# Attention and a gated convolution on one core: the convolution's wrapped columns, and a new order for every instruction

## The chip, the core and the metric

The kernel runs on one core of a Trainium2 chip. The core has five engines that run side by side, each with its own instruction queue that it works off strictly in order: TensorE (PE in the profile; PEld are its weight loads), VectorE (DVE), ScalarE (ACT), GpSimd (POOL) and SyncE (SP). SP issues transfers and does no arithmetic; POOL and ACT issue some as well. An instruction waits on semaphores for what other engines or transfers have to finish first. The metric is the time of one execution on the device, in microseconds (us); lower is better.

## The reference

Two layers follow each other. The first is attention with pooled keys and values, the second a feed-forward block whose hidden values are gated by a convolution along the sequence.

```python
# q, k, v: batch 8, heads 8, sequence 576, head size 64
k_p = k.reshape(B, H, 72, 8, D).mean(axis=3)          # 72 pooled keys per head
v_p = v.reshape(B, H, 72, 8, D).mean(axis=3)
scores = matmul(q, k_p.T) / sqrt(D)
scores -= max(scores, axis=-1)
attn = exp(scores); attn /= sum(attn) + 1e-9
x = matmul(attn, v_p)                                  # heads side by side: 8 x 576 x 512
h = maximum(x @ w_in, 0)                               # 512 -> 1024
conv_out[s] = w[0] * h[s-1] + w[1] * h[s] + w[2] * h[s+1]   # per feature, zeros beyond the ends
out = (h * sigmoid(conv_out)) @ w_out                  # 1024 -> 512
```

Inputs and output are float32; the kernel computes in bf16 with float32 sums.

## The kernel before

Batches are taken in pairs, called groups: g0 holds batches 0 and 1, g3 batches 6 and 7. A group has nine tiles of 128 rows (t0 to t8; t4 is shared by both batches; g0 has a tenth).

*Attention* (`add_att`), per tile: scores on PE (L607 by quarters of the array, L620 with the whole array), maximum on DVE (L633), the maximum taken off on DVE (L645; for g0 on PE, L653), exponential on ACT (L682), a turn of the result (g0 and g1: PE at L692 and a copy at L706; g2 and g3: a transposing transfer from SP), the product with the values on PE (L717), a reciprocal (L730) and the division, on DVE at L745 or as eight narrow ACT instructions at L738. The result is turned again into `xT` (PE and a copy at L762 and L770, or a transfer). Ahead of that, keys are pooled and turned (L431 in halves, L441 in quarters of the array, copies at L456, L483, L504), queries turned (L541, L545, copy at L559), and values folded by DVE in three additions (L511) and spread by a mask (L515).

*Feed-forward* (`add_ffn`), per batch: the first matrix product on PE (L775), a ReLU on ACT into `hT` (L784), and then for each quarter of the work, which is four of the eight blocks of 128 features (`f4`), the convolution in one of two ways.

- On DVE, for the seven quarters in `TAPS` (batches 4 to 6 whole and the first half of batch 7): two instructions per block (L911) add the neighbours, an ACT instruction (L921) squashes.
- On PE, for the other nine quarters (`ffn_conv`, L939): diagonal 64 by 64 matrices times shifted columns of `hT`, in four quarters of the array at once; ACT squashes (L964).

Then DVE multiplies gate and hidden values (L989), and PE makes the output tiles with the second matrix (`add_out`, L997), which ACT or DVE copies out (L1008) for a store.

*Wrapped columns.* The sequence is stored in nine runs of 64 columns, so that the neighbour of the last column of one kind lies at the far end of the tile. `hT` has spare columns on both sides. For batches 4 to 7 (`WRAP`) POOL copies 63 columns to each side (`ffn_wrap`, L859 and L860), two blocks at a time, so that a shifted read is one piece. Where there is no wrap, `conv_todo(False)` cuts the shifted reads into pieces instead. Before, batch 7's second quarter, the last that PE convolves, reads wrapped columns: 24 matmuls per pair of blocks, after POOL's copies.

*The order.* Nothing is scheduled while the kernel is built: `ORDER` lists every operation by its number with the engine it goes to, `FORMS` tells which shape PE uses where there is a choice, and `PLACES` which buffer an operation gets. Numbers of -1 are filler matmuls (L424), of which 40 are used. `Graph.order` reads these lists; since every engine works in order, they set what waits behind what.

*Loads.* POOL issues the loads of queries (L284), keys (L284, L291), values (L317, L320) and weights (L327, L335) in list order, so a load that waits for its buffer holds back those behind it.

```python
        for n in self.ORDER:
            o = spares.pop(0) if n < 0 else self.ops[n // 2]
            o.engine = list(o.engines)[0 if n < 0 else n % 2]
```

Of the kernel before, what the change touches and what calls it, by code (L numbers as in the profile page):

```python
# [12 lines left out]
ACT = mybir.ActivationFunctionType  # L13
# [20 lines left out]
class Graph:  # L34
# [148 lines left out]
def kernel(  # L183
# [1125 lines left out]
    def add_ffn(b, w):  # L1309
# [28 lines left out]
        for f4 in range(n_fb // 4 if b in Graph.WRAP else 0):  # L1338
            n = Graph.WRAPS
            for lo in range(4 * f4, 4 * f4 + 4, n):  # L1340
                o = add({"POOL": (0.6, 1.0, 0, 1.5)[n - 1]}, w, lambda lo=lo, n=n: ffn_wrap(b, lo, lo + n), uses=[htok[b]],
                        after=[o for fb in range(lo, lo + n) for o in relu[fb]] + [ends])
                for fb in range(lo, lo + n):
                    wraps[fb] = o
# [151 lines left out]
```

## Time and profile before

| what | us |
|---|---|
| median of 3 runs | 217.48 (216.86 to 217.99) |
| the profiled execution, whole | 217.29 |
| its span, first to last instruction | 215.4 |
| PE busy | 202.8 |
| DVE busy | 190.8 |
| ACT busy | 164.8 |
| POOL busy | 45.7 |

The span is what the engines' rows cover; the profiled execution's own time is 1.89 us longer. A row of a group names the source line, the engine, the operation, what it writes and reads, the shape and how often; then the busy time in us and the mean length of one in ns, and then idle time just before it with what ended that. A busy PE is not a PE at its peak, since matmuls overlap. A row of the timeline gives start, length and, in brackets, idle time before it.

### The profile page before, as it was taken

What the parts mean: (1) busy time and instruction counts of PE and PEld (TensorE: products, weight loads), DVE (VectorE), ACT (ScalarE), POOL (GpSimd) and SP (SyncE); (2) the same over time, 40 slices, a digit from 0 to 9 for tenths busy, and PEclk for the clock granted to TensorE, in tenths of its full rate; (3) what the DMA queues carried; (4) which work ended last, traced back from release to release, by engine and by line L of the source; (5) the groups of instructions that cost most, each with busy time, mean ns of one, the idle gap of its engine ahead of it and who ended that gap; (6) DMA issues with size and microseconds to landing.
All of it is one profiled execution on the core that took longest, in us unless ns stands there. A gap on an engine that the chain in (4) does not pass through costs nothing.

```text
span 215.4 us, 6639 instructions
## 1 busy us (share of the span) xinstructions
PE 202.8 (94%) x2728; PEld 136.1 (63%) x2728; DVE 190.8 (89%) x338; ACT 164.8 (77%) x331; POOL 45.7 (21%) x78
## 2 busy tenths in 40 slices
PE   4979999999999999989999999999999999989992
PEld 1546778775688877756867775566466556735451
DVE  7779989999999989979999999999999999998521
ACT  2527767998898878977996996999989988968220
POOL 8824130443102012000000142040210411281000
PEclk9999999999999999999999999999999999999999
DMA  6999999999999998965788686565567553320985
GB/s 209 215 205 207 208 205 208 208 207 206 207 248 208 205 141 127 174 150 61 141 116 121 138 115 132 74 139 116 103 134 170 125 109 79 73 46 3 241 257 185
DMA packets 48833, 33.46 MB, mean 155 GB/s; under 512 B 28300, under 2 KB 43812, under 8 KB 48804
## 3 DMA queue, kind: packets, MB, share of 16 engines
q0 software_dynamic: 15216, 15.40, 43.8%
q1 hardware_dynamic: 32592, 16.20, 36.9%
q10 hardware_dynamic: 996, 1.45, 2.4%
q8 instruction: 21, 0.34, 0.6%
q14 instruction: 8, 0.07, 0.1%
HBM read 32.52 MB, written 9.44 MB: 195 GB/s over the span
## 4 chain that ended last, share of the span: by engine, by line
PE 58%; DVE 17%; ACT 9%; issue 3%; POOLq 1%; DMA 1%; POOL 1%; DVEq 0%; ACTq 0%
PE psum L997 23%; PE psum L775 18%; PE psum L717 4%; PE psum L939 4%; DVE negm L633 4%; DVE sd L645 3%; DVE x L745 3%; DVE gT L989 2%; ACT hT L784 2%; PE psum L762 2%; DVE gT L981 2%; ACT gT L964 2%; PE psum L607 2%; PE psum L692 2%; ACT tg L964 1%
## 5 line engine op out<-in xcount | busy, mean ns | idle before, releaser
L775 PE MATMUL psum<-xT,w_in_sb 128*128 128x288 bf16 x512 | 71.6, 286 | 0.5 <-ACT tg L964 0.3
L997 PE MATMUL psum<-w_out_sb,gT 128*128 128x512 bf16 (+1 forms) x296 | 68.0, 374 | 1.3 <-DVE sd L645 1.1
L775 PEld LDWEIGHTS <-w_in_sb 128*128 128x128 bf16 x512 | 48.3, 98 | 16.7 <-issue 1.2
L784 ACT ACTIVATE hT<-psum 128x576 bf16<-128x576 f32 x64 | 41.2, 664 | 8.3 <-PE psum L775 7.8
L997 PEld LDWEIGHTS <-gT 128*128 128x128 bf16 x296 | 27.4, 98 | 28.2 <-DVE sd L645 1.3
L633 DVE TENSOR_REDUCE negm<-psum 128x8 f32<-128x576 f32 (+2 forms) x37 | 27.4, 749 | 3.0 <-PE psum L607 1.6
L859 POOL COPY hT<-hT 128x126 bf16<-128x126 bf16 x16 | 10.6, 661 | 90.0 <-ACT hT L784 73.0
L911 DVE SCALAR_TENSOR_TENSOR tg<-hT,ratio 128x576 f32<-128x576 bf16 x28 | 22.5, 814 | 1.2 <-ACT gT L921 0.5
L911 DVE SCALAR_TENSOR_TENSOR tg<-hT,ratio,tg 128x576 f32<-128x576 bf16 x28 | 22.7, 821 | 0.8
L921 ACT ACTIVATE gT<-tg,ratio 128x576 bf16<-128x576 f32 x28 | 21.4, 790 | 0.5 <-DVE tg L911 0.2
L989 DVE TENSOR_TENSOR gT<-gT,hT 128x2304 bf16<-128x2304 bf16 x16 | 21.3, 1345 | 0.2
L645 DVE TENSOR_TENSOR sd<-psum,negm 128x576 f32<-128x576 f32 x27 | 20.1, 754 | 0.9
L682 ACT ACTIVATE e<-sd 128x576 bf16<-128x576 f32 x27 | 18.8, 701 | 1.8 <-DVE sd L645 1.7
L738 ACT ACTIVATE x<-psum,r 128x64 bf16<-128x64 f32 x80 | 17.6, 341 | 1.7 <-DVE r L730 1.7
L745 DVE TENSOR_TENSOR x<-psum,r 128x512 bf16<-128x512 f32 (+1 forms) x27 | 18.4, 686 | 0.6
L717 PE MATMUL psum<-vm,eT 128*128 128x65 bf16 (+5 forms) x240 | 18.5, 222 | 0.3 <-DMA eT<-e 0.3
L939 PE MATMUL psum<-hT,dw 64*64 64x288 bf16 (+2 forms) x560 | 17.5, 258 | 1.1 <-POOL hT L859 0.7
L717 PEld LDWEIGHTS <-eT 128*128 128x128 bf16 (+1 forms) x240 | 14.8, 100 | 4.0 <-DMA eT<-e 0.6
L939 PEld LDWEIGHTS <-dw 64*64 64x64 bf16 x560 | 13.8, 107 | 5.0 <-issue 4.3
L1008 ACT COPY osb<-psum 128x512 f32<-128x512 f32 x26 | 15.4, 601 | 0.9 <-PE psum L997 0.9
L964 ACT ACTIVATE gT<-psum 128x576 bf16<-128x576 f32 x18 | 11.6, 656 | 5.4 <-PE psum L939 5.4
L424 PE MATMUL psum<-gT 128*128 128x448 bf16 x40 | 12.6, 415 | 2.9 <-DVE gT L1106 2.8
(96 smaller groups left out, 243.1 us busy)
## 6 DMA issues: line engine op xcount, KB each, us to landing
out_dram<-osb SPq DMA_DIRECT2D x54, 128.0 KB, 2.5
v<-in_v_dram POOLq DMA_DIRECT2D x8, 512.0 KB, 14.8
qp<-in_q_dram POOLq DMA_DIRECT2D x7, 576.0 KB, 18.7
kk<-in_k_dram POOLq DMA_DIRECT2D x3, 1152.0 KB, 16.5
out_dram<-qp ACTq DMA_DIRECT2D x10, 128.0 KB, 2.9
hT<-in_k_dram SPq DMA_DIRECT2D x2, 576.0 KB, 5.1
w_in_sb<-in_moe_w_in_dram POOLq DMA_DIRECT2D x2, 512.0 KB, 15.8
w_out_sb<-in_moe_w_out_dram POOLq DMA_DIRECT2D x1, 1024.0 KB, 18.9
```

Of the source, the lines that this page charges most:

```text
L633: nc.vector.tensor_reduce(out=a["m"][0:rows], in_=a["s"][0:rows, :, 0:2 * KW].rearrange("p a (h s) -> p a h s", s=Sp), axis=AX.X, op=OP.ma ...
L645: nc.vector.tensor_tensor(out=a["d"][0:rows], in0=a["s"][0:rows, :, 0:2 * KW].rearrange("p a (h s) -> p a h s", s=Sp), in1=a["m"][0:rows]. ...
L682: nc.scalar.activation(out=dst, in_=src, func=ACT.Exp,)
L717: nc.tensor.matmul(out=a["o"][lo:hi, h // 4, (h % 4) * (D + 1):(h % 4 + x1 - x0) * (D + 1)], lhsT=a["eT"][:, j, lo:hi], rhs=buf("vm", b)[: ...
L745: nc.vector.tensor_tensor(out=a["x"][0:rows].rearrange("p (a h d) -> p a h d", a=2, d=D), in0=ov[:, :, :, 0:D], in1=r[0:rows].unsqueeze(3) ...
L775: nc.tensor.matmul(out=banks(ps)[:, j, 0:SC], lhsT=w_in_block(dc, fb), rhs=buf("xT", g)[:, dc, i * S + j * SC:i * S + (j + 1) * SC], start ...
L784: nc.scalar.activation(out=h_of(b)[:, fb].rearrange("p (a s) -> p a s", a=2), in_=banks(ps)[:, :, 0:SC], func=ACT.Relu, scale=1.0 if (b, f ...
L911: nc.vector.scalar_tensor_tensor(out=acc, in0=h, scalar=w, in1=acc if tap else mid, op0=OP.mult, op1=OP.add)
L921: nc.scalar.activation(out=gate, in_=acc_of(b, fb, ps), func=squash(b, fb), scale=ratio[:, 1, fb:fb + 1])
L939: nc.tensor.matmul(out=banks(pss[r ^ c])[c * D:(c + 1) * D, j, lo:hi], lhsT=dw[r * D:(r + 1) * D, tap * n_fb + fb, :], rhs=hT[r * D:(r + 1 ...
L989: nc.vector.tensor_tensor(out=gate, in0=gate, in1=h_of(b)[:, four], op=OP.mult)
L997: nc.tensor.matmul(out=bank(ps)[0:rows, columns], lhsT=buf("gT", g)[:, fb, t * P:t * P + rows], rhs=w_out_sb[:, fb, columns], start=(fb == 0),
```

## The change

Four edits go together.

1. PE's convolution always uses the cut pieces: batch 7's second quarter goes from 24 to 32 matmuls per pair of blocks and depends on the ReLUs alone.
2. Wraps are made only where DVE convolves, fourteen instead of sixteen.
3. A wrap can be put on ACT; the new order puts three of the fourteen there (batch 4 blocks 6 and 7, batch 6 blocks 6 and 7, batch 7 blocks 2 and 3).
4. `ORDER`, `FORMS` and `PLACES` are new throughout. Beside the sequence of everything, this changes which engine some operations run on, and on POOL's queue the sequence of the loads.

```diff
     ORDER = (
-        0, 12, 10, 24, 16, 4, 44, 28, 8, 36, 14, 32, 46, 40, 64, 38, -1, -1, 21, 3,
...
+        0, 10, 24, 16, 4, 44, 28, 8, 36, 12, 14, 32, 46, -1, -1, -1, -1, -1, -1, 42,
...
-    def ffn_wrap(b, lo, hi):
+    def ffn_wrap(b, lo, hi, copy):
         t = buf("hT", b)[:, lo:hi]
-        nc.gpsimd.tensor_copy(out=t[:, :, 1:TB], in_=t[:, :, S:S + TB - 1])
-        nc.gpsimd.tensor_copy(out=t[:, :, TB + S:TB + S + TB - 1], in_=t[:, :, TB + 1:2 * TB])
+        copy(out=t[:, :, 1:TB], in_=t[:, :, S:S + TB - 1])
+        copy(out=t[:, :, TB + S:TB + S + TB - 1], in_=t[:, :, TB + 1:2 * TB])
...
-        hT, todo = buf("hT", b), conv_todo(b in Graph.WRAP)
+        hT, todo = buf("hT", b), conv_todo(False)
...
         for f4 in range(n_fb // 4 if b in Graph.WRAP else 0):
+            if (b, f4) not in Graph.TAPS and b not in Graph.SIXTEEN:
+                continue
             n = Graph.WRAPS
             for lo in range(4 * f4, 4 * f4 + 4, n):
-                o = add({"POOL": (0.6, 1.0, 0, 1.5)[n - 1]}, w, lambda lo=lo, n=n: ffn_wrap(b, lo, lo + n), uses=[htok[b]],
+                o = add({"POOL": (0.6, 1.0, 0, 1.5)[n - 1], "ACT": 0.43}, w, None, uses=[htok[b]],
                         after=[o for fb in range(lo, lo + n) for o in relu[fb]] + [ends])
+                o.emit = lambda lo=lo, n=n, o=o: ffn_wrap(b, lo, lo + n, nc.gpsimd.tensor_copy if o.engine == "POOL" else nc.scalar.copy)
...
-            conv = add({"PE": 0.64 if b in Graph.WRAP else 0.66}, w + 6 * f2 + Graph.QCONV + nudge("c", 4 * b + f2), lambda f2=f2, cbs=cbs: ffn_conv(b, f2, cbs),
-                       after=([wraps[fbs[0]]] if fbs[0] in wraps else relu[fbs[0]] + relu[fbs[1]]) + dwo, uses=cbs + tg + [htok[b], gtok[g]],
-                       mode=QUARTER, count=48 if b in Graph.WRAP else 64)
+            conv = add({"PE": 0.66}, w + 6 * f2 + Graph.QCONV + nudge("c", 4 * b + f2), lambda f2=f2, cbs=cbs: ffn_conv(b, f2, cbs),
+                       after=relu[fbs[0]] + relu[fbs[1]] + dwo, uses=cbs + tg + [htok[b], gtok[g]],
+                       mode=QUARTER, count=64)
```

What the new order moves, counted in the instructions of both kernels (before, after):

| operation | DVE | ACT |
|---|---|---|
| division of a tile (L745; eight narrow ones at L738) | 25, 23 | 10, 12 tiles |
| turn copy 128x640 (L706) | 7, 3 | 10, 14 |
| turn copy 128x320 (L706) | 0, 1 | 2, 1 |
| key copy 64x288 (L456) | 0, 2 | 2, 0 |
| key copy 128x576 (L504) | 1, 0 | 1, 2 |
| query copy 128x1152 (L559) | 2, 4 | 8, 6 |
| query copy 128x512 (L559) | 1, 0 | 1, 2 |
| output copy 128x512 (L1008, last group) | 3, 4 | 5, 4 |
| wrap copies (L859, L860; before all on POOL, 32, after 22) | - | 0, 6 |

On PE: L431 36 to 54, L441 72 to 36, L541 108 to 126, L545 216 to 180, L607 320 to 352, L620 64 to 56, L939 560 to 576 matmuls. POOL's loads before: values 0, rest of queries 0, keys 1, queries 1, input weights, queries 2, values 1, values 2, keys 2 and 3, queries 3, queries 4, output weights, values 3, values 4, and on. After: rest of queries 0, values 0, keys 1, queries 1, queries 2, input weights, values 1, keys 2 and 3, queries 3, queries 4, output weights, values 2, values 3, keys 4 and 5, and on. At the end of DVE's queue the products of batch 6 (L989) are now followed by six of batch 7's convolution steps (L911) instead of five.

More of the change, by code (lines that the diff above doesn't have):

```diff
@@ L72 @@
     ORDER = (
[54 rows of a table removed]
[54 rows of a table added]
     )
     FORMS = (
-        0, 0, 0, 0, 1, 1, 1, 0, 0, 0, 1, 1, 1, 0, 1, 0, 1, 0, 0, 0, 0, 1, 1, 1, 1, 0, 0, 1, 0, 0, 0, 1, 1, 1, 1, 1, 1, 1, 0, 0,
+        1, 1, 0, 0, 1, 0, 1, 0, 0, 1, 0, 0, 1, 1, 0, 0, 1, 0, 0, 0, 0, 1, 1, 1, 0, 0, 0, 1, 1, 0, 0, 1, 1, 1, 0, 1, 1, 1, 0, 1,
     )
     PLACES = (
[18 rows of a table removed]
[18 rows of a table added]
     )
```

142 rows, old and new, of tables (ORDER, PLACES) are left out of this document.

## The prediction

> **What bounds the kernel now.** I read the page's first part, then busy time by stretch, then the timeline around the last wait, then the groups by shape.
>
> ```profile
> span 215.4 us, 6639 instructions
> PE 202.8 (94%) x2728; PEld 136.1 (63%) x2728; DVE 190.8 (89%) x338; ACT 164.8 (77%) x331; POOL 45.7 (21%) x78
> ```
>
> TensorE (PE) and VectorE (DVE) are both nearly full over the span, so neither share alone names the bound. The next rows give stretches: start and end, then busy time of PE, its weight loads, DVE, ScalarE (ACT) and GpSimd (POOL).
>
> ```profile
> 0.00:27.00 27.00, 22.53 (x335) 14.31 (x335) 22.28 (x62) 13.78 (x24) 13.87 (x29) 1.00 1.08 209
> 27.00:125.00 98.00, 95.72 (x1712) 71.37 (x1709) 91.89 (x167) 82.31 (x154) 13.29 (x19) 1.00 1.04 169
> 125.00:190.00 65.00, 64.47 (x550) 40.37 (x549) 63.22 (x94) 59.55 (x140) 14.54 (x26) 1.00 0.56 116
> 190.00:195.00 5.00, 3.96 (x54) 2.12 (x56) 4.58 (x5) 2.51 (x5) 3.98 (x4) 1.00 0.00 0
> 195.00:201.40 6.40, 6.40 (x42) 2.93 (x31) 6.08 (x9) 4.93 (x9) 0.00 (x0) 1.00 0.31 72
> 201.40:215.40 14.00, 9.73 (x53) 5.00 (x51) 2.76 (x5) 1.76 (x3) 0.00 (x0) 1.00 0.78 230
> ```
>
> From 27 to 190 us PE idles 2.28 + 0.53 = 2.8 us and DVE 6.1 + 1.8 = 7.9 us; ACT has 15.7 us free until 125 and 5.5 us from there to 190. The granted clock is 1.00 in every stretch, so it plays no part. The next rows are the timeline at the end (start, length, what; in brackets the idle time before it and who ended it).
>
> ```profile
> 190.41 2.62 DVE L989 TENSOR_TENSOR gT<-gT,hT 128x2304 bf16<-128x2304 bf16 x2
> 190.44 2.74 POOL L859 COPY hT<-hT 128x126 bf16<-128x126 bf16 x1 [0.88 <-ACT hT L784]
> 193.13 0.81 POOL L860 COPY hT<-hT 128x126 bf16<-128x126 bf16 x1
> 193.23 0.43 PE L939 MATMUL psum<-hT,dw 64*64 64x288 bf16 x6 [0.71 <-POOL hT L859]
> 193.99 1.41 PE L939 MATMUL psum<-hT,dw 64*64 64x288 bf16 x38 [0.33 <-POOL hT L860]
> 194.12 0.29 POOL L860 COPY hT<-hT 128x126 bf16<-128x126 bf16 x1
> 194.21 0.82 DVE L911 SCALAR_TENSOR_TENSOR tg<-hT,ratio 128x576 f32<-128x576 bf16 x1 [0.42 <-POOL hT L859]
> 195.41 15.72 PE L997 MATMUL psum<-w_out_sb,gT 128*128 128x512 bf16 x80
> 198.72 2.63 DVE L989 TENSOR_TENSOR gT<-gT,hT 128x2304 bf16<-128x2304 bf16 x2
> ```
>
> Two paths reach the end together. PE runs its last 80 output matmuls without a break until 195.41 + 15.72 = 211.13; a copy and a store fill the remaining 4.27 us. The last five tiles are 40 of 72 full matmuls' worth (16 of the 80 are half wide), 8.73 us, so PE reaches them at 202.40. They need DVE's last gate products, which end at 198.72 + 2.63 = 201.35. DVE is thus only 1.05 us ahead of PE: a gain must be made on both.
>
> **The change, part by part.** The sum is against this execution: 215.4 + 1.89 around the span = 217.29 us, 0.19 below the median of 217.48.
>
> *The convolution.* Only the last quarter (batch 7, features 512 to 1023) still used wrapped columns on PE. Its two convolutions go from 24 to 32 matmuls each, with the same columns of result. The wrapped ones took 1.41 us for 38, 37 ns each, so 24 take 0.89; the unwrapped ones follow:
>
> ```profile
> 42.50 0.92 PE L939 MATMUL psum<-hT,dw 64*64 64x288 bf16 x32
> ```
>
> So 0.92 against 0.89, +0.06 for two; I take 0.1, with ends 0 and 0.5 (a further eight at 29 ns each, twice). [...]
>
> *Its wrap copies go.* The convolution waits for ACT's activations alone. The two PE waits above, 0.71 + 0.33 = 1.04 us, and DVE's 0.42 us go. Late next is the last activation on ACT, behind one wrap, two squashings and a copy; PE has half an output tile and a convolution (1.7 us) to cover them.
>
> *The other wraps.* Fourteen remain, eleven on POOL and three on ACT. A POOL copy takes 0.29 us alone and 2.74 beside DVE's products. [...] Five fewer pairs on POOL free nothing on DVE that these rows show; I take 0. Those on ACT follow ACT's own ReLUs and wait for no other engine; behind each stand squashings and ReLUs, whose delay is in rival A.
>
> *Work moved from DVE to ACT* (counts from the two engine orders, lengths from these groups, mean ns after the comma):
>
> ```profile
> L745 DVE TENSOR_TENSOR x<-psum,r 128x512 bf16<-128x512 f32 x25 | 17.0, 686 | 0.5
> L706 DVE COPY eT<-psum 128x640 bf16<-128x640 bf16 x7 | 3.4, 482 | 0.2 <-PE psum L692 0.2
> L1008 DVE COPY qp<-psum 128x512 f32<-128x512 f32 x3 | 2.0, 689 | 5.1 <-DMA out_dram<-qp 5.1
> L559 DVE COPY qT<-psum 128x1152 bf16<-128x1152 bf16 x2 | 1.5, 748 | 0.0
> L504 DVE CAST kT<-psum 128x576 bf16<-128x576 f32 x1 | 0.8, 751 | 0.0
> L559 DVE COPY qT<-psum 128x512 bf16<-128x512 bf16 x1 | 0.4, 418 | 0.0
> L738 ACT ACTIVATE x<-psum,r 128x64 bf16<-128x64 f32 x80 | 17.6, 341 | 1.7 <-DVE r L730 1.7
> L706 ACT COPY eT<-psum 128x640 bf16<-128x640 bf16 x10 | 6.7, 696 | 2.2 <-PE psum L692 2.0
> L559 ACT COPY qT<-psum 128x1152 bf16<-128x1152 bf16 x8 | 9.0, 1128 | 0.1
> L483 ACT CAST kT<-psum 64x288 bf16<-64x288 f32 x8 | 3.0, 391 | 0.1
> L921 ACT ACTIVATE gT<-tg,ratio 128x576 bf16<-128x576 f32 x28 | 21.4, 790 | 0.5 <-DVE tg L911 0.2
> ```
>
> DVE before its last product: two divisions less (-1.37), four turn copies less (-1.93), one short one more (+0.30, by half the width of 482 plus a little), one key copy less (-0.75), two 64x288 key copies more (+0.90; this shape is not on DVE before, ends 0.39 and 0.75 each, I take 0.45 as the nearest row is ACT's same shape), two query copies more and one short one less (+1.50 - 0.42). Sum -1.77, with ends -1.9 and -1.2. The extra output copy (0.69) lies after the last product.
> ACT: sixteen narrow divisions more (17.6/80 = 0.22 each, +3.5), four turn copies (+2.8), six wrap copies (between 0.22 and 0.39 each, 0.3, +1.8), two query copies less (-2.3), smaller ones -0.6: +5.2 us. The cover is the 21 us that ACT has free from 27 to 190; without it each of these microseconds would be paid.
>
> *PE's choice of shapes* (keys and queries turned in halves or quarters, scores by rows):
>
> ```profile
> L431 PE MATMUL psum<-gT,kk 128*64 128x144 bf16 x36 | 1.5, 229 | 0.0
> L441 PE MATMUL psum<-gT,kk 64*64 64x72 bf16 x72 | 0.9, 198 | 0.0
> L541 PE MATMUL psum<-ident,qp 128*64 128x128 bf16 x108 | 4.3, 227 | 1.5 <-DMA qp<-in_q_dram 1.3
> L545 PE MATMUL psum<-ident,qp 64*64 64x64 bf16 x216 | 2.9, 195 | 0.1
> L607 PE MATMUL psum<-kT,qT 64*64 64x72 bf16 x320 | 6.0, 199 | 0.0
> L620 PE MATMUL psum<-kT,qT 128*128 128x144 bf16 x64 | 6.5, 226 | 0.2 <-ACT gT L964 0.2
> ```
>
> Busy time over count gives the price: +18 of L431 (0.75), -36 of L441 (-0.45), +18 of L541 (0.72), -36 of L545 (-0.48), +32 of L607 (0.60), -8 of L620 (-0.81): +0.33 us. The 40 filler matmuls stay. In the tail two stores move from ACT's queue to SP's; the last tile keeps one store on each queue per half, so I leave the 4.27 us as they are.
>
> *The start.* On POOL's queue the rest of batch 0's queries now goes ahead of its values, and DVE's first three score maxima ahead of the first fold of the values.
>
> ```profile
> 11.94 1.35 DVE L511 TENSOR_TENSOR v<-v 128x1280 bf16<-128x1280 bf16 x2 [1.74 <-DMA v<-in_v_dram]
> 15.35 1.42 DVE L633 TENSOR_REDUCE negm<-psum 128x8 bf16<-128x576 f32 x2 [0.35 <-PE psum L620]
> ```
>
> DVE's wait of 1.74 us for the values goes; late next are the scores of the first tile, which waited behind it for about as long. Between 0 and 1.74 + 0.35 = 2.1, I take 0.6, nearer the low end since PE and ACT must first make those scores.
>
> *The loads.* Batch 2's values are issued after the output weights instead of before batch 3's queries; batch 2's queries ahead of the input weights.
>
> ```profile
> 50.32 0.74 POOL L284 DMA_DIRECT2D qp<-in_q_dram  x1 [1.46 <-DMA w_out_sb<-in_moe_w_out_dram]
> 53.25 0.74 POOL L317 DMA_DIRECT2D v<-in_v_dram  x1 [2.19 <-DMA v<-in_v_dram]
> 55.01 0.69 DVE L745 TENSOR_TENSOR x<-psum,r 128x512 bf16<-128x512 f32 x1
> ```
>
> Up to batch 3's values both orders have loaded the same bytes: output weights are down by 50.3 us and those values by 53.2. Batch 2's now take the place between, so they land at about 50.3. DVE folds them where the division at 55.01 stood, about 2.2 us earlier by then (a lighter queue and the start), 52.8. The margin is 2.5 us, so I take 0; it costs what goes beyond.
>
> *The sum.* DVE's last product: 201.35 - 1.77 - 0.6 - 0.42 + 0.35 (it now waits for two squashings of 0.79 that end late) = 198.9. PE's arrival at the last five tiles: 202.40 - 1.04 - 0.6 + 0.1 + 0.33 = 201.2, and less again by what it idled on a late DVE from 27 to 190: between 0 and 2.8, half, 1.4, giving 199.8. PE is the later. 199.8 + 8.73 + 4.27 + 1.89 = **214.7 us**. If PE wins back none of its idle time, 216.1; if all of it, DVE decides: 198.9 + 0.1 + 8.73 + 4.27 + 1.89 = 213.9. With the start at its best on both, 212.4. A change of 0.5%, 1.1 us, is about what the three runs (216.86 to 217.99) can tell from none.
>
> **The rivals.**
> *A, ACT becomes the late engine (slower).* Its extra 5.2 us stand in the same queue as the ReLUs that PE and DVE wait for, and from 125 to 190 it is 92% busy already. For it: 59.55 of 65 us. Against: most of the extra work lies before 125 us, where 15.7 us are free. It decides where more than half of the 5.2 us, the 2.6 us that the sum gains, comes on the path: all of it gives 214.7 + 5.2 = 219.9, three quarters 218.6. Chance 0.24.
> *B, batch 2's values come late (slower).* The queue waits, ahead of them, for query buffers that PE must empty. If that issue slips, DVE stands still in order, and everything behind it. It decides from a landing at 52.8 + 2.6 = 55.4; at 58 us the time is 219.9. The rows have the landing 5 us before that. Chance 0.08.
> *C, what the waits gave up is idle elsewhere (no change).* All orders are new, and DVE's 7.9 us and PE's 2.8 us of idle time from 27 to 190 are in many short waits, none of which carries over. With 2.5 us more of them on the path, 217.2. Chance 0.15.
>
> **How the numbers follow.** The forecast, 212.4 to 216.1, has 0.53; A 0.24, B 0.08, C 0.15. C is within 0.5%, A and B are slower. The likeliest case gives the time. For eight in ten the range leaves out a tenth at each end: low 212.5, high 220.0, where A and B in full end.
>
> **What would show it.** Right: no POOL wait before the last convolution, 64 matmuls there in under 2 us; DVE busy about 1.1 us less in all and its first 1.74 us wait gone; ACT busy near 170; the last 40 output matmuls starting near 199.8. Wrong: a DVE wait of over 2 us on values or scores between 40 and 80 us (B); DVE or PE rows idle on ACT's ReLUs for over 3 us in all (A); a stop of over 1 us ahead of the last five tiles would say that DVE, not PE, sets the end.

## The result, and the profile after

The changed kernel takes 218.93 us (median of 12 runs; 218.64, and 217.94 to 219.99, without the first) against 217.57 us for the kernel before beside it: a ratio of 1.0066, 95% interval 1.0037 to 1.0096. It is slower, and the whole interval lies above 1; 214.7 us was forecast. On a second chip the unchanged file gave 219.18 us and 1.0109 (1.0066 to 1.0151). The first of the twelve, which was the profiled one, took 336.67 us at a mean granted clock of 0.56 and is left out of the ratio, so the trace read here is that of another execution of the same kernel, 218.56 us.

Lines of its page: span, busy times, and the shares of the chain that ended last.

```profile
span 216.6 us, 6657 instructions
PE 203.6 (94%) x2732; PEld 136.8 (63%) x2732; DVE 189.6 (88%) x336; ACT 168.5 (78%) x353; POOL 38.9 (18%) x68
PE 58%; ACT 12%; DVE 12%; DMA 10%; issue 3%; POOL 1%; SPq 0%; DVEq 0%; ACTq 0%
```

Transfers make 10% of the chain, before 1%: 4% are transfers of turned exponentials, 4% loads of values, 2% transfers of the turned output `xT`. Busy time by stretch, columns as before:

```profile
0.00:27.00 27.00, 24.29 (x373) 15.19 (x374) 22.03 (x61) 15.11 (x25) 11.20 (x22) 1.00 1.08 204
27.00:125.00 98.00, 93.52 (x1647) 69.85 (x1646) 88.81 (x161) 82.87 (x167) 15.08 (x24) 1.00 1.04 172
125.00:190.00 65.00, 64.91 (x558) 41.10 (x557) 63.67 (x96) 60.59 (x147) 12.63 (x22) 1.00 0.59 114
190.00:195.00 5.00, 5.00 (x82) 2.98 (x81) 5.00 (x6) 4.92 (x10) 0.00 (x0) 1.00 0.23 52
195.00:201.40 6.40, 6.40 (x31) 2.92 (x30) 5.98 (x9) 3.24 (x6) 0.00 (x0) 1.00 0.19 44
```

From 190 us on PE's rows are full and no wait for POOL is left, as forecast. The loss is in the second row: PE idles 98.00 - 93.52 = 4.48 us there, before 2.28, and DVE 9.19, before 6.11. The chain shows where (start, length, what):

```profile
93.99 4.38 DMA eT<-e
98.37 0.05 issue
98.42 1.28 PE psum L717 x18
...
103.18 3.57 DMA eT<-e
106.75 0.05 issue
106.80 0.53 PE psum L717 x6
...
200.73 1.37 DVE gT L989
202.10 0.05 issue
202.15 8.84 PE psum L997 x48
```

The products with the values wait for turned exponentials. PE's timeline has the same two stops (idle time before in brackets):

```profile
98.42 1.28 PE L717 MATMUL psum<-vm,eT 128*128 128x130 bf16 x18 [2.19 <-DMA eT<-e]
106.80 0.53 PE L717 MATMUL psum<-vm,eT 128*128 128x130 bf16 x6 [1.23 <-DMA eT<-e]
```

SP issues these transfers; its own timeline, first of the changed kernel, then of the one before (L553 sends a batch's queries, L701 an exponential tile, L1020 stores):

```profile
85.00 1.12 SPq L1020 DMA_DIRECT2D out_dram<-osb  x2
86.31 7.58 SPq L553 DMA_TRANSPOSE qT<-qp  x1
93.99 3.49 SPq L701 DMA_TRANSPOSE eT<-e  x2
97.54 1.22 SPq L1020 DMA_DIRECT2D out_dram<-osb  x2
98.87 2.80 SPq L553 DMA_TRANSPOSE qT<-qp  x1
```

```profile
86.27 1.11 SPq L1020 DMA_DIRECT2D out_dram<-osb  x2
87.49 2.72 SPq L701 DMA_TRANSPOSE eT<-e  x2
90.31 4.08 SPq L553 DMA_TRANSPOSE qT<-qp  x1
98.27 3.27 SPq L701 DMA_TRANSPOSE eT<-e  x2
```

Before, two exponential tiles went out first, at 87.49, and the queries behind them. After, the queries of batch 6 stand first, and to issue their transfer holds SP for 7.58 us; the same instruction needs 2.80 us at 98.87. What ran at that time is on POOL's queue:

```profile
65.96 0.79 POOL L284 DMA_DIRECT2D qp<-in_q_dram  x1
74.06 1.01 POOL L291 DMA_DIRECT2D kk<-in_k_dram  x1 [7.31 <-PE psum L470]
82.53 0.77 POOL L317 DMA_DIRECT2D v<-in_v_dram  x1 [7.46 <-DVE vm L515]
83.29 0.56 POOL L320 DMA_DIRECT2D v<-in_v_dram  x1
83.85 0.76 POOL L284 DMA_DIRECT2D qp<-in_q_dram  x1
```

The row at 83.85, now the last load of all, is the one of batch 7's queries. Before, it went out at 50.32. Now it stands behind the values of batch 7 (82.53), which wait 7.46 us for their buffer. The list of transfers gives it 10.1 us to land (KB, then us), so until 93.95, just as SP comes free:

```profile
qp<-in_q_dram POOLq DMA_DIRECT2D x1, 576.0 KB, 10.1
```

The end lost time too. SP's timeline there, after and before (`qp` holds the last group's output tiles):

```profile
192.34 3.92 SPq L1020 DMA_DIRECT2D out_dram<-osb  x4
201.68 1.11 SPq L1020 DMA_DIRECT2D out_dram<-qp  x2
202.83 4.75 SPq L1020 DMA_DIRECT2D out_dram<-osb  x6
207.80 6.10 SPq L1020 DMA_DIRECT2D out_dram<-qp  x8
```

```profile
198.15 1.11 SPq L1020 DMA_DIRECT2D out_dram<-qp  x2
199.30 6.99 SPq L1020 DMA_DIRECT2D out_dram<-osb  x10
206.39 5.86 SPq L1020 DMA_DIRECT2D out_dram<-qp  x6
```

After, SP issues nothing from 196.26 to 201.68: it waits for a tile's copy, and finished tiles of group 2 stand behind. From 201.6 us on, 26 transfers are left to issue on SP and ACT, before 22. PE's last matmul ends at 210.97 (before 211.13), the span 5.63 us later, before 4.22.

The sum of the traced execution beside the forecast: PE reaches the last five tiles at 202.15 instead of 199.8 (+2.35), they take 8.82 instead of 8.73, the end behind them 5.63 instead of 4.27 (+1.36), and 1.96 lies around the span instead of 1.89: 218.56 against 214.7.

### The profile page after: what moved, and what is told of

Same layout as the page of the kernel before. It is cut to its first block, busy times and chain, and to the rows that moved or that the text cites. A ratio compares the mean times of both kernels' runs of the same rounds, so it can differ in the third digit from the quotient of the medians.

```text
span 334.7 us, 6637 instructions
## 1 busy us (share of the span) xinstructions
PE 324.9 (97%) x2712; PEld 183.6 (55%) x2732; DVE 193.5 (58%) x336; ACT 175.3 (52%) x353; POOL 34.1 (10%) x68
## 4 chain that ended last, share of the span: by engine, by line
PE 97%; issue 1%; ACT 0%; DVE 0%; DVEq 0%
PE psum L775 33%; PE psum L997 32%; PE psum L939 7%; PE psum L717 7%; PE psum L424 4%; PE psum L692 3%; PE psum L762 2%; PE psum L541 2%; PE psum L620 2%; PE psum L607 2%; PE psum L653 1%; PE psum L431 1%; PE psum L545 1%; PE psum L493 0%; PE psum L470 0%
## 5 line engine op out<-in xcount | busy, mean ns | idle before, releaser
L775 PE MATMUL psum<-xT,w_in_sb 128*128 128x288 bf16 x512 | 118.9, 415 | 0.0
L997 PE MATMUL psum<-w_out_sb,gT 128*128 128x512 bf16 (+1 forms) x276 | 111.6, 569 | 4.0 <-issue 2.9
L775 PEld LDWEIGHTS <-w_in_sb 128*128 128x128 bf16 x512 | 66.2, 134 | 40.0 <-issue 7.1
L997 PEld LDWEIGHTS <-gT 128*128 128x128 bf16 x296 | 37.1, 129 | 59.6 <-issue 55.7
L730 DVE RECIPROCAL r<-psum 128x8 f32<-128x8 f32 (+1 forms) x37 | 7.6, 206 | 52.2 <-PE psum L717 32.0
L911 DVE SCALAR_TENSOR_TENSOR tg<-hT,ratio 128x576 f32<-128x576 bf16 x28 | 22.2, 816 | 15.0 <-ACT gT L921 12.8
L1008 ACT COPY osb<-psum 128x512 f32<-128x512 f32 x26 | 15.2, 589 | 27.3 <-PE psum L997 21.5
L717 PE MATMUL psum<-vm,eT 128*128 128x65 bf16 (+5 forms) x240 | 27.8, 284 | 0.0
L717 PEld LDWEIGHTS <-eT 128*128 128x128 bf16 (+1 forms) x240 | 21.4, 126 | 7.3 <-issue 3.6
L939 PE MATMUL psum<-hT,dw 64*64 64x288 bf16 (+2 forms) x576 | 25.3, 343 | 0.0
L738 ACT ACTIVATE x<-psum,r 128x64 bf16<-128x64 f32 x96 | 20.9, 334 | 5.3 <-DVE r L730 3.7
L911 DVE SCALAR_TENSOR_TENSOR tg<-hT,ratio,tg 128x576 f32<-128x576 bf16 x28 | 22.3, 812 | 0.6
L989 DVE TENSOR_TENSOR gT<-gT,hT 128x2304 bf16<-128x2304 bf16 x16 | 21.4, 1346 | 0.5 <-ACT gT L921 0.3
L939 PEld LDWEIGHTS <-dw 64*64 64x64 bf16 x576 | 16.9, 130 | 8.1 <-issue 3.4
L859 POOL COPY hT<-hT 128x126 bf16<-128x126 bf16 x11 | 3.9, 353 | 160.4 <-ACT hT L784 127.4
L745 DVE TENSOR_TENSOR x<-psum,r 128x512 bf16<-128x512 f32 (+1 forms) x25 | 16.9, 684 | 0.5
```

The costliest lines, as they stand in the source:

```text
L717: nc.tensor.matmul(out=a["o"][lo:hi, h // 4, (h % 4) * (D + 1):(h % 4 + x1 - x0) * (D + 1)], lhsT=a["eT"][:, j, lo:hi], rhs=buf("vm", b)[: ...
L738: nc.scalar.activation(out=a["x"][0:rows, n * D:(n + 1) * D], in_=ov[:, n // 4, n % 4, 0:D], func=ACT.Identity, scale=r[0:rows, n // 4, n ...
L775: nc.tensor.matmul(out=banks(ps)[:, j, 0:SC], lhsT=w_in_block(dc, fb), rhs=buf("xT", g)[:, dc, i * S + j * SC:i * S + (j + 1) * SC], start ...
L911: nc.vector.scalar_tensor_tensor(out=acc, in0=h, scalar=w, in1=acc if tap else mid, op0=OP.mult, op1=OP.add)
L939: nc.tensor.matmul(out=banks(pss[r ^ c])[c * D:(c + 1) * D, j, lo:hi], lhsT=dw[r * D:(r + 1) * D, tap * n_fb + fb, :], rhs=hT[r * D:(r + 1 ...
L989: nc.vector.tensor_tensor(out=gate, in0=gate, in1=h_of(b)[:, four], op=OP.mult)
```

## The experiments

Every kernel was timed beside the kernel before. The order is edited where `Graph.order` returns it: `done` is the list of operations in the sequence of `ORDER`, with shapes and buffers already given, so to move an entry changes its place on its own engine's queue and nothing else. The added lines shift line numbers by one to four (L701 becomes L702 to L705).

**The changed kernel once more, the convolution alone, the wraps back on POOL.**

```diff
-        hT, todo = buf("hT", b), conv_todo(b in Graph.WRAP)
+        hT, todo = buf("hT", b), conv_todo(False)
...
-                       after=([wraps[fbs[0]]] if fbs[0] in wraps else relu[fbs[0]] + relu[fbs[1]]) + dwo, uses=cbs + tg + [htok[b], gtok[g]],
+                       after=relu[fbs[0]] + relu[fbs[1]] + dwo, uses=cbs + tg + [htok[b], gtok[g]],
```

The second kernel is the one before with this, and with batch 7's second pair of wraps not made. The third is the changed one with three numbers of `ORDER` less by one (1319, 1777, 1985), which puts its three wraps of ACT on POOL.

> The changed kernel once more, unchanged, for its trace. Theory W (the start): the time that was lost lies in the first 27 us, where PE reaches its full clock later than before (before: from 7.65 us on); the granted clock's mean over the span is then below 1.00 by about 0.01, and what comes after 27 us takes no longer than before. Theory S (new stalls): the clock is full from the same time as before, and DVE and PE idle 2 to 4 us more between 27 and 190 us. Theory A (ACT late): those idle times are ended by ACT.

> The kernel before with edit 1 alone: the last quarter's convolution on unwrapped columns, waiting for the ReLUs, its four wrap copies left out, every order as before. The prediction's terms give 1.04 us of PE waits gone and 0.1 us of longer convolutions, so about 0.9 us less where PE sets the end (216.6 beside 217.5); a tie says that DVE, 1.05 us ahead, or the wait for something else takes the place of the POOL waits.

> The changed kernel with its three ACT wraps on POOL, order otherwise the same. Theory A: ACT is 1.8 us lighter, so the time falls by 0.5 to 1.8 us against the changed kernel. Theories W and S: no difference over 0.5 us, or a little slower through POOL's copies beside DVE's two-input instructions.

The changed kernel: 219.18 us. Of the three theories on it, S holds: the granted clock is 1.00 in the rows above, PE idles 1.8 and DVE 2.6 us more from 27 to 190 us, and transfers, not ACT, end PE's two long stops. The convolution alone: **215.78 us, 0.9931 (0.9904 to 0.9958)**, faster than both kernels. The wraps on POOL: 219.46 us, 1.0120 (1.0081 to 1.0160). So the edit of the convolution keeps its gain, which wraps run on ACT is not the cause, and the new order costs 3 to 4 us.

**The queries later on SP's queue.** In the changed kernel the transfer of batch 6's queries moves behind four exponential tiles, or behind two:

```diff
+        done.insert(558, done.pop(507))
```

```diff
+        done.insert(530, done.pop(507))
```

The third kernel is the opposite, in the kernel with the convolution alone: batch 7's queries ahead of two exponential tiles.

```diff
+        done.insert(517, done.pop(528))
```

> The changed kernel with one transfer moved on SP's queue: the transposing transfer of batch 6's queries stands behind the four exponential tiles of group 2 (t2, t1, t0, t3) instead of ahead of them; every other instruction keeps its place. Theory 1 (the queries' transfer holds SP from 86.31 to 93.89 us, so the exponentials' transfers go out at 93.99 instead of about 86.4, and PE stands 2.19 us and then 1.23 us): the first two go out at 86 to 88, both stops of PE fall under 0.5 us, the clock's drop goes with them, 215.5 to 216.8 us, ratio to the kernel before 0.991 to 0.997. Theory 2 (the DMA engines are full of the loads of v7 and q7 until 94, whatever stands first): the exponentials go out early but land after 96 all the same, a stop of 1.5 us or more stays, 218.3 to 219.2 us. Theory 3 (the loss is spread over the new orders): 218.6 to 219.5 us, and what is won at 96 is lost before 125.

> As the last, but batch 6's queries go directly behind the first two exponential tiles (t2, t1), so ahead of batch 7's queries and of the exponentials t0 and t3. Theory 1: the first stop goes (2.19 to under 0.5 us); the second (1.23 us) stays in so far as two transfers of queries of 2.8 to 4 us each stand ahead of t0 and t3: 216.0 to 217.8 us. Theory 2: 218.3 to 219.2 us, as above. Theory 3: 218.6 to 219.5 us.

> The kernel before with the edit of the convolution alone (215.78 us), and the suspected cause put into it: batch 7's queries stand ahead of the exponentials t1 and t2 on SP's queue instead of behind them. Theory 1: the exponentials go out 3 to 4 us later (their issue behind the transfer of the queries, at about 91.5 instead of 87.8), PE stops on them for 1 to 2.5 us at 97 to 100, where it did not stop: 216.8 to 218.5 us. Theory 2: here no load of queries is in flight at that time, so nothing changes: 215.2 to 216.4 us. Theory 3: 215.2 to 216.4 us.

Behind four tiles: 217.71 us, 1.0023 (0.9997 to 1.0049). Behind two: 216.94 us, 0.9985 (0.9964 to 1.0006). The first stop is gone in both, but either keeps one: the first kernel a new one behind, the second the old second one, longer. PE's timeline of the first and of the second:

```profile
119.01 0.66 PE L776 MATMUL psum<-xT,w_in_sb 128*128 128x288 bf16 x4 [1.99 <-DMA xT<-x]
```

```profile
105.30 0.53 PE L718 MATMUL psum<-vm,eT 128*128 128x130 bf16 x6 [1.79 <-DMA eT<-e]
```

SP's queue is so full from 85 to 122 us that what is moved out of the way is late itself. The order on SP's queue matters, and theory 2 (nothing helps while the load runs) falls, since tiles sent first land in time (the first 8.5 to 9.3 us after its issue, before 5.7); but it isn't all. In the other kernel the queries ahead cost little: 216.31 us, 0.9947 (0.9925 to 0.9970), where 216.8 to 218.5 was expected. SP was held 5.04 us and the tiles went out at 92.71, but there PE took them up only at 97.74, just after the second had landed (97.47), without a stop. Theory 1 had the mechanism and overlooked that slack.

**The load earlier on POOL's queue.** In the changed kernel batch 7's queries are loaded right behind batch 6's; then the same with the queries behind two exponential tiles; then with two finished output tiles stored at about 59 us instead of 93 and some 120; and the convolution alone once more beside them.

```diff
+        for to, at in ((489, 491),):
+            done.insert(to, done.pop(at))
```

```diff
+        for to, at in ((489, 491), (530, 507)):
+            done.insert(to, done.pop(at))
```

```diff
+        for to, at in ((489, 491), (530, 507), (478, 555), (479, 685)):
+            done.insert(to, done.pop(at))
```

> The changed kernel with one load moved on POOL's queue: batch 7's queries are loaded right behind batch 6's (from about 66.7 us on) instead of behind the keys of pair 3 and the values of batch 7 (83.85 to 93.99 us); SP's queue is as in the changed kernel, batch 6's queries ahead of the exponentials. Theory 1a (the transfer of the queries holds SP long because that load fills the DMA engines at the same time): SP is held from about 86.4 for 4 to 5.2 us instead of 7.58, as long as where no such load ran (4.08 in the kernel before, 5.15 with the queries put early), the first exponentials go out at 90.5 to 91.7 and land at 95 to 96.5, PE's stop of 2.19 us falls under 0.8, and the time to 216.6 to 217.8 us. Theory 1b (the order on SP's queue alone counts): the hold stays above 7 us and the time at 218.6 to 219.4 us.

> Both edits: batch 7's queries loaded early, and batch 6's sent behind the first two exponentials. Theory 1a: exponentials out at 86 to 88 and landed by 93, both transfers of queries gone by 96, so that the exponentials t0 and t3 go out at 97 to 99 and neither stop of PE is over 0.5 us: 215.2 to 216.6 us. Theory 1b: as with the order alone, 216.5 to 217.4 us. If what is lost elsewhere in the new orders decides, 216.8 to 217.8 us.

> As the last, and the two finished output tiles t2 and t1 of group 0 are stored at about 54 us, where SP has nothing to do, instead of at 95 and 122 us between the transposing transfers. Theory: four issues of 0.64 us leave SP's full stretch from 85 to 125 us, so what PE and DVE still wait there for the transfers of the outputs goes: 0 to 0.7 us less than the last, 214.8 to 216.4 us. Rival: the stores slow the loads of 54 to 70 us by 1.3 us in all, and scores of group 2 wait for them: 0 to 1.5 us more than the last.

> The kernel before with the edit of the convolution alone, once more beside the three others: 215.2 to 216.3 us.

One load moved by two places on its queue: **215.58 us, 0.9928 (0.9900 to 0.9955)**, 3.4 us less than the changed kernel by the medians, 3.0 to 3.9 by the ratios to the kernel before. With the queries moved too: 215.25 us, 0.9898 (0.9871 to 0.9925). With the stores: 215.08 us, 0.9897 (0.9868 to 0.9926). The convolution alone: 216.14 us, 0.9928 (0.9901 to 0.9955). SP's timeline and PE's two products with the load early, SP's queue otherwise as in the changed kernel:

```profile
86.98 5.43 SPq L555 DMA_TRANSPOSE qT<-qp  x1
92.51 3.47 SPq L703 DMA_TRANSPOSE eT<-e  x2
```

```profile
96.65 1.40 PE L719 MATMUL psum<-vm,eT 128*128 128x130 bf16 x18 [0.18 <-DMA eT<-e]
105.14 0.53 PE L719 MATMUL psum<-vm,eT 128*128 128x130 bf16 x6 [1.21 <-DMA eT<-e]
```

The hold falls from 7.58 to 5.43 us (4 to 5.2 expected) and the stop from 2.19 to 0.18, as theory 1a had it; theory 1b falls. The traced execution, at 217.29 us, is the slowest of its twelve; the median is better than expected. In the third kernel both stops are gone, and with them most of PE's idle time (27 to 125 us, 125 to 190 us):

```profile
27.00:125.00 98.00, 96.92 (x1683) 72.78 (x1683) 92.70 (x170) 87.07 (x180) 16.12 (x26) 1.00 1.02 177
125.00:190.00 65.00, 64.92 (x604) 40.99 (x603) 63.79 (x92) 60.51 (x142) 11.56 (x20) 1.00 0.55 107
```

**The cause put into the other kernel.** The convolution alone, with the load of batch 6's queries moved behind the values of batch 7; then with batch 7's queries ahead of two tiles on SP's queue as well.

```diff
+        for to, at in ((505, 279),):
+            done.insert(to, done.pop(at))
```

```diff
+        for to, at in ((505, 279), (517, 528)):
+            done.insert(to, done.pop(at))
```

> The kernel before with the edit of the convolution alone (215.8 to 216.1 us), and one half of the cause put into it: the load of batch 6's queries, which there nothing needs before 104 us, moves on POOL's queue behind the values of batch 7, so that it runs from about 85 to 95 us, as the load of batch 7's queries does in the changed kernel. SP's queue stays, the exponentials ahead of batch 7's queries. Theory (both halves are needed): the exponentials go out at 87.8 as before and land 1 to 3 us later, before PE takes them up at 98; 215.6 to 216.8 us. Rival (the late load alone makes the stop): a stop of PE of over 1 us between 96 and 104, 217 to 219 us.

> Both halves: the late load, and batch 7's queries ahead of the first two exponentials on SP's queue (which alone gave 216.31 us, no stop of PE, and a hold of 5.1 us). Theory (the load lengthens the hold): SP is held by the transfer of the queries until about 95, for over 7 us, the exponentials go out at 95 to 96.5 and land at 99.5 to 101, PE stops for 1.3 to 3 us at 98 to 101: 217.0 to 218.8 us. Rival (the hold does not depend on the load): 5.1 us and 216.0 to 216.8 us.

The late load alone: 218.46 us, 1.0068 (1.0038 to 1.0097), so 2.3 to 2.7 us are lost, and the theory that both halves are needed falls. With both: 219.98 us, 1.0139 (1.0109 to 1.0169), over the 217.0 to 218.8 expected; SP is held for 7.99 us, as expected. But the stop isn't where I put it. The exponentials caused none; PE stood earlier (first kernel):

```profile
93.71 1.14 PE L999 MATMUL psum<-w_out_sb,gT 128*128 128x512 bf16 x4 [2.06 <-DVE eT L708]
```

The row names a DVE copy, but that ended at 92.92, and nothing that the trace shows was outstanding after it. What lands in that time is a packet of 16 KB on q8, a queue that the page calls `instruction`. With the convolution alone the packet ends at 91.48 and PE goes on at 92.89; with the late load 92.38 and 93.71; with both halves 93.04 and 94.56. In the last two PE goes on 1.3 and 1.5 us after its packet, while DVE's work before it ends within 0.15 us of where it did; in the first a DVE result at 92.64 explains the wait as well. In the four other traces of the old order PE stops at the same place, for 1.14 to 1.48 us, and goes on 1.20 to 1.59 us after that packet. I take the packet to hold instructions of PE (last section) and to be the cause of the longer stops; no run shows the first, and the second is argued from the traces and not tried by itself. So the late load has one price that is shown, and perhaps a second: with the queries put ahead, their transfer holds SP longer (7.99 us against 5.04), and, if the packet is the cause, what PE waits for ends 0.90 us later (92.38 against 91.48). The half clock that follows the stop in the traced execution (last section) is a further one, but not the whole rest: the three executions of the late load alone with a granted clock of 1.000 still took 217.46 to 218.39 us. What makes up the remainder was not followed.

**The end.** First the two stores that the change moved from ACT to SP: back on ACT in the changed kernel, back on ACT in the kernel of 215.08 us, and moved to SP in the one with the convolution alone.

```diff
+        for at in (1065, 1069):
+            done[at].engine = "ACT"
```

```diff
+        for at in (1061, 1064):
+            done[at].engine = "SP"
```

> The changed kernel with two stores of the last group (tiles t4 and t5) issued by ACT, as in the kernel before, instead of by SP; no other edit. Theory (SP's queue sets the end: its last eight issues run from 207.80 to 213.90 us, PE is done at 210.97, and the span ends 5.63 us behind PE instead of 4.22): the end comes 1.0 to 1.5 us earlier, 217.4 to 218.2 us, and the span ends 4.1 to 4.6 us behind PE's last matmul. Rival (the transfers themselves set the end, whoever issues them): 5.3 to 5.9 us behind PE, 218.6 to 219.4 us.

> The kernel with the load of batch 7's queries early, batch 6's queries behind the first two exponentials and two stores early (215.08 us, the span ending 5.9 us behind PE), and the two stores of the last group on ACT. Theory: 1.2 to 1.7 us less, 213.3 to 214.0 us, within 1.4 us of the 214.7 that was forecast. Rival: 214.8 to 215.4 us.

> The kernel before with the edit of the convolution alone (215.78 and 216.14 us), and the stores of the last group's t4 and t5 issued by SP instead of ACT. Theory: SP's queue ends 1.0 to 1.6 us later, 216.8 to 217.7 us. Rival: 215.6 to 216.4 us.

219.26 us (1.0103, 1.0066 to 1.0140), 215.18 us (0.9909, 0.9873 to 0.9945) and 217.08 us (0.9986, 0.9959 to 1.0013). In the order of before the two stores cost about 1 us, and the end grows from 4.35 to 5.12 us behind PE; in the new order to take them back wins nothing, and the end stays at 5.52 and 5.63 us. The theory falls there: something else holds SP. Then the stores that stand ready behind SP's wait, moved ahead of it, in the changed kernel and in the kernel of 215.08 us:

```diff
+        for to, at in ((1047, 1049), (1048, 1055)):
+            done.insert(to, done.pop(at))
```

> The changed kernel with two stores of group 2 (t7 and t3, copied by about 192 us) moved ahead of the store of group 3's t1 on SP's queue, which waits 5.8 us for a copy on ACT that ends at 201.6. Theory (what stands in SP's queue behind that wait makes the end late: 26 issues are left at 201.6 us, 22 in the kernel before): four issues go out before 201 us, the span ends 4.2 to 4.8 us behind PE's last matmul instead of 5.63, 217.6 to 218.4 us. Rival (the end has another cause): 5.4 to 5.8 us, 218.6 to 219.4 us.

> The kernel with the load early, batch 6's queries behind the first two exponentials and the two stores of group 0 early (215.08 us, 5.89 us behind PE), and the same two stores of group 2 moved. Theory: 4.2 to 5.0 us behind PE, 213.6 to 214.4 us. Rival: 214.8 to 215.4 us.

218.16 us (1.0033, 1.0013 to 1.0053) and **213.92 us (0.9834, 0.9805 to 0.9863)**: 0.8 to 1.0 and 1.2 us less, and in both the end is 4.84 us behind PE. SP's timeline of the second:

```profile
188.96 5.36 SPq L1022 DMA_DIRECT2D out_dram<-osb  x8
198.29 1.11 SPq L1022 DMA_DIRECT2D out_dram<-qp  x2
199.44 1.44 SPq L1022 DMA_DIRECT2D out_dram<-osb  x2
```

Eight transfers instead of four go out before the wait. This kernel, the change with six entries of two queues moved (one load, one transfer of queries, four stores), is the fastest of all.

## Why the prediction was wrong

- **The loads**: this step failed. It followed the new sequence on POOL's queue as far as batch 3's values and took 0. What it should have priced stood further back: batch 7's queries went behind the values of batch 7, which wait for a buffer, and so from 50.32 to 83.85 us, into the stretch where SP sends transposing transfers. (The row at 50.32 that the prediction shows is that very load; it was read there only for the time at which the output weights had landed.) SP's queue got no step but the two stores of the tail, though there the queries had moved ahead of the exponentials. What the runs showed in place of the 0: SP held for 7.58 us, and PE stopped for 2.19 and 1.23 us. Put back, the load alone wins 3.4 us, and both together 3.7. The part that was worked out, batch 2's values, held: they landed at 50.5 and 50.9 us (forecast 50.3), and rival B did not occur.
- **What PE idled from 27 to 190** (2.8 us before): forecast to fall to 1.4, it rose to 4.48 + 0.09 = 4.57. With load, queries and stores mended it is 1.08 + 0.08 = 1.16. The two stops, 3.42 us, ate the term. That without them it comes out near 1.4 is luck in part, since the half was a guess between 0 and all.
- **The end**: "so I leave the 4.27 us as they are" failed; it is 5.63. The step counted stores per queue and not what waits ahead of them. The wait of SP for a copy, with ready stores behind, costs 0.8 to 1.2 us; the other 0.6 us (4.84 against 4.22) is open.
- **The convolution and its wraps**: on PE the terms give 1.04 us of waits gone and 0.1 paid, so 0.9; the two runs of this edit alone gave 0.69% and 0.72%, about 1.5 us. In the first one's trace PE's idle time falls by 1.03 us from 190 to 201.4 us, as forecast, and by 0.34 from 125 to 190. Its 64 matmuls take under 2 us as said, and no wait for POOL is left (changed kernel):

```profile
191.40 1.91 PE L939 MATMUL psum<-hT,dw 64*64 64x288 bf16 x64
193.24 17.73 PE L997 MATMUL psum<-w_out_sb,gT 128*128 128x512 bf16 x88
```

- **The other wraps**: 0 forecast, 219.46 against 219.18 us measured. Right within what those runs can tell.
- **DVE to ACT**: DVE is busy 1.2 us less (forecast 1.1). On ACT the groups came as forecast (narrow divisions +3.5, turn copies +2.8, wraps +2.0), but its busy time grew by 3.7 us instead of 5.2. Rival A did not occur: with the loads mended, ACT keeps its 3.7 us and the kernel is 1% faster than before.
- **The start**: DVE's wait of 1.74 us for the values is gone, but no sign of 0.6 us won on DVE. The values land later (13.94 against 11.53 us), DVE does other work meanwhile, and up to 27 us it is busy 22.03 us, before 22.28. PE is busy 1.76 us more there, 1.08 of it without the filler matmuls, so for PE the term may hold; no run tried it alone.
- **Which engine ends last**: PE, said the sum; that failed too. The traces have PE's last five tiles start 0.06 us after DVE's last product (202.09 and 202.15; with load, queries and stores mended 198.28 and 198.34). PE's matmuls before them start 0.22 us apart, the last at 201.67, so PE stands about 0.26 us for DVE there (the same in the mended kernel), which the merged rows above do not show. DVE sets the end, by little: its last product was forecast for 198.9.
- **The rivals**: C, that what the waits give up is idle elsewhere, comes nearest. Its price (2.5 us) was short of the 4.2 us missed, and its picture (many short waits) was wrong: two long ones within ten microseconds.

With both queues mended the time is 213.92 us, 0.8 below the forecast and inside the likeliest case's range of 212.4 to 216.1. That is another kernel, and some of the nearness is luck: the convolution gave more than its term, the end is 4.84 instead of 4.27, and DVE sets it. But it says that the work on the engines was priced about right; what was not looked at is two queues that issue transfers.

## What to carry to other kernels

Where a change rewrites an order, compare the whole sequence of every queue that issues transfers, to its last entry, and ask of each entry that moved behind a wait what it will then run beside. A queue that issues transfers is an engine like the others: what stands ready behind a wait, or behind an issue that takes long, is late even when nothing computes (here behind an issue of 7.58 us, and behind a wait that cost 0.8 to 1.2 us of the whole). If a large edit loses where its small core should win, run the core alone first, then move single entries of the new order: here one load was worth as much as the whole loss.

## What the runs showed of the hardware

**A transposing transfer took longer to issue while loads were in flight.** In 18 traces (all but the first measurement's), two transfers of queries each, it held SP for 2.67 to 3.04 us in 18 cases with no load in flight (3.41 and 3.59 in two more), for 3.52 to 5.43 in the nine where batch 7's values were in flight or had landed at most 0.11 us before, and for 7.58 to 7.99 in the five that began with a load of queries in flight as well. These five ended 0.11 to 0.17 us before that load landed; the two that began with 3.5 and 3.7 us of it to come took 4.58 and 4.60. Moving that one load took the hold from 7.58 to 5.43 us in the new order and from 5.04 to 7.99 in the old. In the changed kernel the issue was 7.58 of the transfer's 11.2 us to landing.

**Half the clock followed a stop of PE of 2 us in four traces.** The late load alone, from 94 to 98 us, behind its stop of 2.06 us:

```profile
94.00:98.00 4.00, 4.00 (x56) 1.96 (x54) 2.62 (x3) 1.19 (x2) 0.00 (x0) 0.57 1.22 223
```

The granted clock is 0.57 there and 1.00 around it. Four traces have such a stretch: it begins 0.4 to 1.3 us after the end of a stop of 1.99 to 2.78 us, and lasts 3.41 us at a clock of 0.50 (in stretches of 4 us that take it in, the granted clock is 0.57 here, 0.74 and 0.84 with both halves of the cause, 0.68 and 0.89 with the wraps on POOL, which comes to 3.4 us each time). Three others, with stops of 2.19 to 2.50 us, have none. In the kernels whose trace has a stop of 1.99 us or more, 28 of 70 executions had a mean granted clock of 0.990 or less; in the other kernels of the experiments, longest stop 1.79 us, one of 86, in the kernel with that stop (both counts without the two executions at 0.66 or less throughout). The bound is rough: the execution shown here has 0.992. For the changed kernel it parts spans of 217.2 to 219.5 us from 216.1 to 216.8, some 1.2 us in about half of its executions, and may be why mending the load won more in the median than its trace shows. What decides whether a stop is followed by such a stretch, no run shows.

**A queue named `instruction` moves 16 KB packets while the kernel runs.** A line of the page, alike in all these kernels (packets, MB, share of 16 engines):

```profile
q8 instruction: 21, 0.34, 0.6%
```

0.34 MB in 21 packets are 16 KB each. That they hold PE's instructions is inferred and not shown: PE and its weight loads are 5,464 of the 6,657 instructions. With the load in flight one of them ended 0.90 us later than with the convolution alone (92.38 against 91.48), and PE's stop there was 0.89 us longer (2.06 against 1.17).
